# Identity products beside attention's transposes, for the first two units of heads instead of the first five

## The chip, the cores and the metric

The program runs on one core of one Trainium2 chip. The metric is device time in microseconds (us). The core's engines are named as the profile names them: PE (TensorE matmul) with PEld (its weight load), DVE (VectorE), ACT (ScalarE), POOL (GpSimd) and SP (SyncE, which here only issues transfers; its queue is SPq).

## What is computed

Attention with a local or a strided mask, then a two-layer MLP on its output, then a routed mixture of eight experts. Cut to what matters here:

```python
scores = scale * np.matmul(q, k.transpose(0, 1, 3, 2))     # 4 batches, 8 heads, 576 rows, 64 wide
scores = np.where(masks[None], scores, -1e9)               # heads 0-3 local, heads 4-7 strided
attn = np.exp(scores - scores.max(-1, keepdims=True))
attn = attn / (attn.sum(-1, keepdims=True) + 1e-9)
x = np.matmul(attn, v)                                     # to (2304, 512)
h = x @ w_in; x = np.maximum(0.01 * h, h) @ w_out          # w_in 512x2048, w_out 2048x512
out = moe2(x)                                              # 8 experts, capacity 288 tokens each
```

## The kernel before

**Attention.** A unit `u` (0 to 15) is two heads of one batch; `u % 4` below 2 means local heads, else strided ones. Each unit has two groups `g`, and `attention()` walks the 32 pairs (u, g) as a pipeline: at step s it transposes q and k of the next unit (`a_tr`, L122), makes the scores of pair s (`a_qk`, L166, with the mask and minimum on DVE in L157 and the exponential on ACT in L159), normalises them (`a_norm`, the sums on DVE in L178 and L179, the products on POOL in L181), transposes the probabilities of pair s-2 (`a_pt`, L194, for each of the two heads h, copied out of PSUM by ACT in L196) and multiplies those of pair s-3 with V (`a_pv`, L209). q, k and V of later units are loaded through SP's queue (L97, L106 to L110) into buffers that come free when earlier units have been used.

**The identity products.** In `a_pt`, ahead of the transposes of one pair and one head, PE multiplies the identity with itself three times (L192) into `p[:, 3]`, a column block that nothing reads. L193 transposes `n` blocks (3, or 2 for the first strided group) into the blocks below it. Before the change this is done for units 0 to 4. `a_qk` has a like product for units 0 and 1 (L169), which stays. A product of this kind is two instructions in the trace (each fp32 matmul of L192, L122, L166, L194 and L209 runs as two).

**What stands beside it.** From the start, 32 halves of the two MLP weights are loaded by POOL's queue (L306 for `w_in`, L309 for `w_out`, 512 KB each, two buffers) and turned from fp64 into fp32 by ACT (L320) and DVE (L322 to L324): `convert(n)`. When the first eight pairs of attention are written out in the program, the MLP begins: block 0 of tokens, with `g1` (L373 to L375, into the PSUM tile `p1`, one buffer), `g2` (L397 to L399), and `split` (L349 on ACT, L352 on POOL) for the weights' high and low parts; pieces of attention are written between its pieces.

**What sets the order.** Each engine runs its instructions in the order of its own queue. That order isn't the one written: the tile framework's scheduler picks it when the program is built, by its own estimate of durations. So an edit of a few instructions can move their neighbours on every engine.

Of the kernel before, what the change touches and what calls it, by code (L numbers as in the profile page):

```python
# [26 lines left out]
def body(ctx, tc, q, k, v, w_in, w_out, w_gate, w1, w2, out):  # L27
# [109 lines left out]
    def group(u, g):  # L137

        if u % 4 < 2:
            return 96, 128, [(96 * i, 96 * i, ml0 if i == 0 else ml, i) for i in range(3 * g, 3 * g + 3)]  # L140
        w = 18 * RG[2 * g][1]
        return w, w, [(18 * RG[i][0], 32 + 18 * RG[i][0], msf, i) for i in ((0, 1), (2, 3, 4))[g]]
# [41 lines left out]
    def a_pt(u, g, h):  # L184
        nq, nk, tl = group(u, g)
        n = len(tl)
        if h == 0:
            PT[u, g] = at.tile([128, 2, 3, 128], F32, name="pt", tag="pt")
        tag = "p2" if u < 5 and h else "pT"
        p = ps.tile([128, 4, 128], F32, name="pP", tag=tag, bufs=BUFS[tag])  # L190
        for _ in range(3 if u < 5 else 0):
            nc.tensor.matmul(p[:, 3], ident, ident, start=True, stop=True)  # L192
        for i in range(n):  # L193
            nc.tensor.transpose(p[:nk, i, :nq], SC[u, g][0][:nq, h, i, :nk], ident[:nq, :nq])  # L194
        if h or EARLY[0]:
            nc.scalar.activation(PT[u, g][:nk, h, :n, :nq], p[:nk, :n, :nq], AF.Copy)  # L196
        else:
            nc.vector.tensor_copy(PT[u, g][:nk, h, :n, :nq], p[:nk, :n, :nq])
# [40 lines left out]
    def attention():  # L239
# [9 lines left out]
        for s in range(n + 3):  # L249
# [10 lines left out]
            if mid:  # L260
                a_pt(*mid, 0)
                yield
# [12 lines left out]
            if mid:  # L275
                a_pt(*mid, 1)
                yield
# [704 lines left out]
```

## Time and profile before

| | us |
|---|---|
| median of 3 runs | 918.29 (913.65 to 925.14) |
| the profiled execution | 926.83 |
| its span in the trace | 925.1 |
| PE busy in the span | 860.2 (93%) |
| ACT / DVE / POOL busy | 441.9 / 563.3 / 471.5 |

The profiled execution is 8.5 us over the median of the runs, and 1.7 us of it lie around its span. Spans on PE are modelled: an instruction that is shown as 272 ns long is followed by the next of its kind well before those are over, so the cost of a row is better read from one start to the next. [...]

### The profile page before, as it was taken

The page shows a single profiled execution, that of the slowest core. Times are in us where ns is not written, and L with a number is a line of the kernel's source. Part 1 is how long each engine was busy: PE and PEld are TensorE (multiplying, and loading weights), DVE is VectorE, ACT ScalarE, POOL GpSimd, SP SyncE. Part 2 cuts the span into 40 slices and gives each one's busy share as a digit, 9 for nine tenths or more (in the row PEclk, how much of TensorE's full clock was granted, in tenths as well). Part 3 has the DMA queues.
Part 4 walks back from the last instruction along what each step waited for, and adds up shares of the span by engine and source line. Part 5 has one row for each costly group of instructions (what it writes and reads, how often), then busy time and mean ns, then how long its engine had stood idle before and what let it go on. Part 6 is the DMA issues. An engine that isn't in the chain of part 4 may idle for free.

```text
span 925.1 us, 16905 instructions
## 1 busy us (share of the span) xinstructions
PE 860.2 (93%) x6274; PEld 726.1 (78%) x6274; DVE 563.3 (61%) x1543; ACT 441.9 (48%) x1095; POOL 471.5 (51%) x394
## 2 busy tenths in 40 slices
PE   7889998899999999999999999978998989897994
PEld 4777766587887888778898877658998989797994
DVE  6777889856446445554555556566877767675330
ACT  5778667464446445454455423324435434243531
POOL 3645646564555556555655445745446263426621
PEclk9789999999999999999999999987999999798997
DMA  8596554320111100100000002325356362425710
GB/s 183 142 200 157 141 144 124 119 61 5 36 26 53 43 14 2 47 1 1 35 1 1 1 1 80 114 67 177 129 154 185 102 182 95 141 92 154 213 35 26
DMA packets 86450, 80.59 MB, mean 87 GB/s; under 512 B 65376, under 2 KB 65376, under 8 KB 86368
## 3 DMA queue, kind: packets, MB, share of 16 engines
q1 hardware_dynamic: 78688, 53.30, 21.1%
q0 software_dynamic: 7680, 26.22, 9.3%
q8 instruction: 49, 0.80, 0.4%
q14 instruction: 33, 0.27, 0.1%
HBM read 70.06 MB, written 9.44 MB: 86 GB/s over the span
## 4 chain that ended last, share of the span: by engine, by line
PE 64%; DMA 10%; DVE 9%; issue 7%; POOL 4%; ACT 4%; SPq 1%; POOLq 0%; ACTq 0%; DVEq 0%
PE p L373 5%; PE p L397 5%; DMA raw<-in_moe_w_dram 4%; PE p L375 4%; PE p L374 4%; PE p L399 4%; PE p L398 4%; PE g L859 3%; PE g L860 3%; PE g L861 3%; PE p L536 2%; PE q L896 2%; PE p L538 2%; PE pS L166 2%; PE p L537 2%
## 5 line engine op out<-in xcount | busy, mean ns | idle before, releaser
L352 POOL TENSOR_TENSOR lo<-WO,hi 128x512 fp32r<-128x512 f32 x96 | 126.6, 1319 | 95.1 <-ACT hi L349 94.9
L352 POOL TENSOR_TENSOR lo<-WI,hi 128x512 fp32r<-128x512 f32 x96 | 126.9, 1323 | 90.1 <-DVE hi L351 58.3
L801 POOL TENSOR_TENSOR wlo<-raw,whi 128x1024 fp32r<-128x1024 f32 x40 | 95.8, 2410 | 113.9 <-ACT whi L800 113.3
L373 PE MATMUL p<-xh,hi 128*128 128x384 f32 x256 | 98.1, 383 | 5.5 <-DVE g L382 5.5
L349 ACT ACTIVATE hi<-WO 128x512 fp32r<-128x512 f32 x96 | 60.5, 630 | 88.2 <-PE q L898 43.7
L375 PE MATMUL p<-xh,lo 128*128 128x384 f32 x256 | 86.9, 339 | 1.4 <-POOL lo L352 1.4
L800 ACT ACTIVATE whi<-raw 128x1024 fp32r<-128x1024 f32 x64 | 66.1, 1055 | 44.4 <-DMA raw<-in_moe_w_dram 39.2
L374 PE MATMUL p<-xl,hi 128*128 128x384 f32 x256 | 86.6, 338 | 0.6 <-DVE xl L234 0.6
L397 PE MATMUL p<-hi,gh 128*128 128x512 f32 x192 | 82.8, 431 | 0.8 <-ACT gh L383 0.8
L859 PE MATMUL g<-hh,whi 128*128 128x288 f32 x256 | 81.4, 319 | 0.5 <-ACT hh L843 0.5
L860 PE MATMUL g<-hl,whi 128*128 128x288 f32 x256 | 79.0, 309 | 0.1
L861 PE MATMUL g<-hh,wlo 128*128 128x288 f32 x256 | 78.7, 307 | 0.0
L836 PE MATMUL g<-exh,whi 128*128 128x288 f32 x256 | 78.4, 307 | 0.0
L837 PE MATMUL g<-exl,whi 128*128 128x288 f32 x256 | 77.4, 303 | 0.0
L838 PE MATMUL g<-exh,wlo 128*128 128x288 f32 x256 | 77.2, 302 | 0.0
L399 PE MATMUL p<-hi,gl 128*128 128x512 f32 x192 | 75.7, 394 | 1.3 <-DVE gl L384 1.3
L159 ACT ACTIVATE sc<-sc,mx 96x128 f32<-96x128 f32 (+2 forms) x176 | 67.6, 386 | 16.6 <-DVE mx L157 16.6
L398 PE MATMUL p<-lo,gh 128*128 128x512 f32 x192 | 75.2, 392 | 0.0
L373 PEld LDWEIGHTS p<-xh,hi 128*128 128x128 f32 x256 | 48.2, 188 | 16.6 <-DVE g L382 6.8
L181 POOL TENSOR_TENSOR sc<-sc,mx 96x384 f32<-96x384 f32 (+2 forms) x64 | 52.3, 834 | 17.3 <-DVE mx L179 10.2
L381 ACT ACTIVATE g<-p 128x384 f32<-128x384 f32 x64 | 31.1, 486 | 57.0 <-PE p L375 56.7
L351 DVE CAST hi<-WI 128x512 fp32r<-128x512 f32 x59 | 26.8, 454 | 46.1 <-PE p L374 35.9
(203 smaller groups left out, 2257.5 us busy)
## 6 DMA issues: line engine op xcount, KB each, us to landing
raw<-in_moe_w_dram SPq DMA_DIRECT2D x64, 512.0 KB
wraw<-in_moe_w_in_dram POOLq DMA_DIRECT2D x16, 512.0 KB
wraw<-in_moe_w_out_dram POOLq DMA_DIRECT2D x16, 512.0 KB
rawq<-in_q_dram SPq DMA_DIRECT2D x32, 144.0 KB
rawk<-in_k_dram SPq DMA_DIRECT2D x32, 144.0 KB
x2d<-x SPq DMA_DIRECT2D x18, 256.0 KB
vt<-in_v_dram SPq DMA_DIRECT2D x16, 160.0 KB
vt<-in_v_dram SPq DMA_DIRECT2D x48, 27.0 KB
```

The costliest lines, as they stand in the source:

```text
L352: nc.gpsimd.tensor_sub(lo, src, hi.bitcast(F32))
L373: nc.tensor.matmul(p1, wh[:, cs], xh[:, c], start=(c == 0), stop=False)
L374: nc.tensor.matmul(p1, wh[:, cs], xl[:, c], start=False, stop=False)
L375: nc.tensor.matmul(p1, wl[:, cs], xh[:, c], start=False, stop=(c == 3))
L397: nc.tensor.matmul(p2[t], gh[:, s], oh, start=(f == 0), stop=False)
L398: nc.tensor.matmul(p2[t], gh[:, s], ol, start=False, stop=False)
L399: nc.tensor.matmul(p2[t], gl[:, s], oh, start=False, stop=(f == 15))
L801: (nc.vector if n in (1, 5, 7) else nc.gpsimd).tensor_sub(lo, raw, hi.bitcast(F32))
L836: nc.tensor.matmul(p, wh, xh[:, c], start=(c == 0), stop=False)
L859: nc.tensor.matmul(p, wh, hh[:, j], start=(j == 0), stop=False)
L860: nc.tensor.matmul(p, wh, hl[:, j], start=False, stop=False)
L861: nc.tensor.matmul(p, wl, hh[:, j], start=False, stop=(j == 7))
```

## The change

```diff
@@ a_pt(u, g, h)
         tag = "p2" if u < 5 and h else "pT"
         p = ps.tile([128, 4, 128], F32, name="pP", tag=tag, bufs=BUFS[tag])
-        for _ in range(3 if u < 5 else 0):
+        for _ in range(3 if u < 2 else 0):
             nc.tensor.matmul(p[:, 3], ident, ident, start=True, stop=True)
         for i in range(n):
             nc.tensor.transpose(p[:nk, i, :nq], SC[u, g][0][:nq, h, i, :nk], ident[:nq, :nq])
```

For units 2, 3 and 4, two groups and two heads each, three products go: 36 products. The PSUM tile that they wrote keeps its size, its tag and its place. The loads, the transposes and the copies are the same in number.

The order on PE, at the transposes of units 2 and 3 that follow each other some 46 us after the start (L194 with 108 and 126 rows are strided groups; `pT` is a transpose of q or k, `pP` one of probabilities):

```order
-L192 MATMUL pP<-ident 128x128 x3
 L194 MATMUL pP<-ident,sc 108x108 x3
 L122 MATMUL pT<-ident,rawq 128x96 x2
-L192 MATMUL pP<-ident 128x128 x3
 L194 MATMUL pP<-ident,sc 126x126 x2
```

Here two sets of three products are gone and nothing else has moved.

The order on PE a little later, between the product with V of unit 2's second group and that of unit 3's first (`pS` are scores). Before:

```order
L192 MATMUL pP<-ident 128x128
L122 MATMUL pT<-ident,rawq 128x96 x2
L122 MATMUL pT<-ident,rawk 128x96 x2
L166 MATMUL pS_883<-qk 96x128
L166 MATMUL pS_884<-qk 96x128
L166 MATMUL pS_883<-qk 96x128
L166 MATMUL pS_884<-qk 96x128
L192 MATMUL pP<-ident 128x128 x4
L194 MATMUL pP<-ident,sc 108x108 x3
L209 MATMUL pX<-pt,vt 64x126 x4
```

With the change:

```order
L194 MATMUL pP<-ident,sc 128x96 x3
L122 MATMUL pT<-ident,rawq 128x96 x2
L122 MATMUL pT<-ident,rawk 128x96 x2
L166 MATMUL pS_859<-qk 96x128
L194 MATMUL pP<-ident,sc 108x108 x3
L166 MATMUL pS_860<-qk 96x128
L166 MATMUL pS_859<-qk 96x128
L209 MATMUL pX<-pt,vt 64x126 x3
```

Five products are gone from the piece; the transposes of 108 rows have moved ahead of three of the four scores, and those of unit 4's first group and head, which stood below, now stand ahead of the transposes of q and k.

On SP's queue one of two loads of a later unit's q has moved behind the six loads of V that followed it:

```order
-L97 DMA rawq<-in_q_dram 96x6x64 x2
+L97 DMA rawq<-in_q_dram 96x6x64
 L108 DMA vt<-in_v_dram 96x64
```

Behind the first eighty or so microseconds the order of every engine is as it was.

## Rows read from the trace of the kernel before

**Rows 1.** The page's head and the first of its busy times.

```profile
span 925.1 us, 16905 instructions
PE 860.2 (93%) x6274; PEld 726.1 (78%) x6274; DVE 563.3 (61%) x1543; ACT 441.9 (48%) x1095; POOL 471.5 (51%) x394
```

**Rows 2.** Busy time by engine in five stretches, granted clock, DMA share, GB/s.

```profile
core 0: us, PE busy (x) PEld busy (x) DVE busy (x) ACT busy (x) POOL busy (x), PEclk, DMA share, GB/s
40.00:60.00 20.00, 16.81 (x172) 14.20 (x170) 14.10 (x70) 16.31 (x66) 8.40 (x14) 1.00 0.92 208
60.00:74.00 14.00, 13.64 (x101) 10.51 (x101) 10.04 (x39) 10.88 (x40) 6.29 (x9) 0.76 0.66 153
81.00:119.00 38.00, 37.44 (x242) 27.60 (x242) 32.20 (x76) 25.70 (x75) 24.46 (x27) 1.00 0.62 156
126.00:190.00 64.00, 56.28 (x352) 40.76 (x351) 54.98 (x126) 39.30 (x110) 37.31 (x37) 1.00 0.38 111
190.00:560.00 370.00, 368.12 (x2457) 301.59 (x2456) 194.04 (x522) 176.12 (x440) 200.58 (x168) 1.00 0.08 21
```

**Rows 3.** L192 on PE: 40 to 81 us, then the whole span (ns min/median/max).

```profile
L192 PE MATMUL pP<-ident 128*128 128x128 f32 x78 | 13.4, 308 | 0.4 <-ACT qk L133 0.2
...
L192 PE MATMUL pP<-ident x120: 272/275/581, 15.0 to 80.8; 128*128 128x128 f32 x120
```

**Rows 4.** PE in order of time: start, us, instructions [idle before <-releaser].

```profile
46.43 0.94 PE L192 MATMUL pP<-ident 128*128 128x128 f32 x6
...
48.82 0.36 PE L122 MATMUL pT<-ident,rawq 96*128 96x96 f32 x2 [1.17 <-DMA rawq<-in_q_dram]
49.01 0.86 PE L192 MATMUL pP<-ident 128*128 128x128 f32 x6
49.71 0.38 PE L194 MATMUL pP<-ident,sc 126*126 126x126 f32 x2
...
85.62 0.36 PE L122 MATMUL pT<-ident,rawk 96*128 96x96 f32 x2 [0.56 <-DMA rawk<-in_k_dram]
```

**Rows 5.** The chain that ended last, 52 to 86 us: start, us, what.

```profile
52.64 6.52 DMA wraw<-in_moe_w_in_dram
59.18 0.66 ACT cg L320
...
61.40 0.53 PE pP L192 x2
...
63.85 2.00 PE pP L192 x8
...
68.11 0.65 PE pP L192 x2
...
70.44 0.87 PE pP L192 x6
...
73.79 0.76 SPq L106
...
81.39 4.09 DMA rawk<-in_k_dram
```

**Rows 6.** ACT in order of time, 60 to 69 us: instructions that waited.

```profile
60.54 0.40 ACT L159 ACTIVATE sc<-sc,mx 96x128 f32<-96x128 f32 x1 [0.43 <-DVE mx L157]
...
65.07 0.67 ACT L320 ACTIVATE cg<-wraw 128x512 f32<-128x512 f32 x1 [0.51 <-DMA wraw<-in_moe_w_out_dram]
...
66.43 0.44 ACT L196 ACTIVATE pt<-pP 108x324 f32<-108x324 f32 x1 [0.69 <-PE pP L194]
...
67.48 0.44 ACT L233 CAST xh<-pX 128x168 fp32r<-128x168 f32 x1 [0.61 <-PE pX L209]
...
68.58 0.40 ACT L159 ACTIVATE sc<-sc,mx 96x128 f32<-96x128 f32 x1 [0.66 <-DVE mx L157]
```

**Rows 7.** PE in single microseconds: us, busy (x), granted clock, DMA share, GB/s.

```profile
59.00:60.00 1.00, 0.00 (x0) 1.00 0.05 11
61.00:62.00 1.00, 0.85 (x5) 0.86 0.75 111
...
67.00:68.00 1.00, 1.00 (x10) 0.50 0.89 315
68.00:69.00 1.00, 1.00 (x9) 0.72 1.20 250
```

## Prediction

> **What bounds the kernel now.** I began with the page's head: PE is busy for 860.2 of 925.1 us [rows 1], so work taken off PE could be worth its full time, if it is taken where PE is what everything waits for. The next view, busy time by stretch, says where that is. From 190 to 560 us PE is busy for 368.12 of 370 us: nothing there waits for anything but PE. From 81 to 119 us it is much the same, 37.44 of 38. From 126 to 190 us PE stands for 7.7 of 64 us, and DVE is the busier engine in proportion to what it can do, 54.98 of 64 us, so there the conversion of the weights has a say [rows 2]. The change touches none of these stretches. It lies in the 40 us ahead of them, and the question is how much earlier the stretch from 81 us begins.
>
> The group of L192 gives the size: between 40 and 81 us it has 78 instructions. 72 of them go (36 products of two instructions each); the other six belong to unit 1 and stay [rows 3]. In that time there are two parts, which the same two views tell apart. From 40 to 60 us PE is busy for 16.81 of 20 us and ACT for 16.31, and the DMA engines for 0.92 of the time, so PE is not alone in setting the pace. From 60 to 74 us PE is busy for 13.64 of 14 us, ACT for 10.88, and PE's granted clock is 0.76 [rows 2]: there PE is the bound. The chain of waits agrees. At 52.64 us it runs through a transfer of weights of 6.52 us, on which ACT's conversion at 59.18 us stood, then through PE with four pieces of L192, and from 73.79 us through SP's queue and a transfer of k that lands at 85.5 us [rows 5].
>
> **The cost of what goes.** A set of three products, six instructions, starts at 49.01 us, and the next instruction starts at 49.71 us: 0.70 us at the upper clock, 0.117 us for an instruction [rows 4]. Twelve instructions run at the lower clock: their three pieces in the chain are 0.53, 2.00 and 0.65 us, 3.18 together [rows 5]. The other 60 cost 60 x 0.117 = 7.0 us. So 10.2 us of PE's time go. That is 1.1% of 926.83 us, and it is the most that the removal alone could give. What is left of it is worked out by part:
>
> 1. *Before 59 us.* Seven sets (42 instructions, 4.9 us). The first of them stand ahead of a transpose at 48.82 us that had already waited 1.17 us for q [rows 4]; without 0.70 us of products at 46.43 us that wait is 1.87 us, and nothing is earlier. The sets behind it end in front of ACT's conversion at 59.18 us, and that waits for a transfer [rows 5]. The copies that PE's product with V needs stand behind it in ACT's queue. Ends: 0, if that transfer lands when it did; 0.7 us, one set, if its issue, which stands behind other work on POOL and DVE, comes earlier too. I take 0.
> 2. *From 60 to 73 us.* The chain holds four pieces of L192: 0.53 + 2.00 + 0.65 + 0.87 = 4.05 us [rows 5]. All of it would be gained if PE alone set the end. But ACT must do its own work there. Its waits in this part are 0.43 + 0.51 + 0.69 + 0.61 + 0.66 = 2.90 us, of which 0.51 is for a transfer [rows 6]. When the products are gone ACT can close the others, 2.39 us, and then it is what PE waits for. Ends: 0, if DVE and the transfer fill the room; 4.05. I take 2.4, since the four others are for PE or for DVE, which stood on PE's scores.
> 3. *From 73 to 86 us.* Two sets, 1.4 us. Behind 73 us the chain is SP's: ten loads of V at about 0.76 us each, then k, whose transfer takes 4.09 us [rows 5]. PE waited 0.56 us for it at 85.62 [rows 4]. Without the products it waits longer. Ends: 0 and 1.4. I take 0. That the loads begin when PE's product with V of unit 3 is done is why the gain of part 2 survives: SP starts as much earlier.
> 4. *The moved instructions.* The transposes of unit 4 that moved up need POOL's products, which needed ACT's and DVE's work; they are late by some tenths or not at all. One load of q moved behind six of V costs nothing by the time of its use. I take 0, with 0.5 us to either side.
> 5. *Behind 86 us.* From 81 to 119 us PE is full, and DVE has 5.8 us idle [rows 2]. A shift of 2.4 us goes through. From 126 to 190 us DVE has 9 us idle in 64, so I keep all of it, with 0 as the other end.
>
> Sum: 926.83 - 2.4 = 924.4 for the profiled execution; from the median of the runs, 918.29 - 2.4 = **915.9 us**.
>
> **The clock.** At 59 us PE was idle for a whole microsecond; from late in 61 us to the middle of 68 us the granted clock was 0.50 (0.86 in the first of these microseconds, 0.72 in the last: 0.28 + 6 + 0.56 = 6.8 us) [rows 7]. So the products did not keep the clock there: they stand in PE's queue like everything else, wait with it, and at that clock they are themselves the longest thing in it. My sum leaves the lower clock where it was. [...]
>
> **The rivals.**
>
> *A, the forecast:* 1 to 4 us are gained, 914 to 917 us. Half the chance, 0.50.
>
> *B, nothing is gained.* The transfer at 59 us and ACT's queue hold the first part, and in the second the lower clock lasts past 68.6 us, to the end of the stretch. PE's work there without the products is 13.64 - 4.05 = 9.6 us; 6.8 - 3.2 = 3.6 us of that ran at the lower clock already, and the 6.0 others would take 12.0 in the worst case, so 15.6 us against 14. If half of this comes true the gain of part 2 is used up: 918 us. For it speak ACT's 10.88 of 14 us and the conversion's own pace; against it, that PE's queue stays full from 60 us on. 0.22.
>
> *C, slower: the products had held the clock from 40 to 60 us,* where it is 1.00 [rows 2]. PE's work there without them is 16.81 - 4.9 = 11.9 us; at the lower clock all through it is 23.8 us against 20, 3.8 us late, and the second stretch adds 15.6 - 14 = 1.6 by B's sum. That is 5.4 us: 923.7 us. It decides from the point where PE's idle time between 46 and 49 us has brought the clock down and it stays down over 50 us. For it: the gaps grow by as much as the products leave. Against it: in the stretch PE has at least 3 us of slack in front of ACT's wait at 59.18 us, so a short fall is hidden. 0.16. [...]
>
> *D, all of it is gained:* 10.2 us, and 1.8 more (half of 3.6) if the lower clock doesn't come: 918.29 - 12 = 906.3; with 8 us, 910. It needs q, the weights and ACT all to come earlier with PE, against parts 1 and 3. 0.12.
>
> **How the numbers follow.** The likeliest is A with 915.9; I say 916. A, B and most of C lie between 912 and 924. The three runs shown spread over 11.5 us, six times the gain that I forecast, so the range must also hold what differs from run to run: 908.5 to 923.5. That leaves out the lower half of D and the upper end of C, some 2 in 10 together. A alone would be 911 to 921. 2% of the time, about what a measurement of this kernel can tell from no change, is 18.4 us. All of the products are 10.2 us and C is 5.4 us, so no case by itself gets there; 0.03 for faster and 0.02 for slower are for what I don't see.
>
> **What the changed profile would show.** L192 has 48 instructions, the last before 45 us. ACT's conversion still waits for weights near 59 us (part 1), and PE's idle time ahead of it is 3 to 5 us longer. SP's ten loads of V of unit 6, which began shortly before 73.79 us, begin near 71 (part 2), and the wait for k at about 83 us is 1.5 to 2 us long (part 3). From 81 to 119 us all is the same, some 2.4 us earlier. The forecast is wrong if the granted clock falls between 46 and 58 us or stays at 0.50 beyond the loads of V (B, C), or if the weights at 59 us come several us earlier (D).

## The result: 0.7% slower, and the profile after

| | before | with the change |
|---|---|---|
| median of 22 runs, us | 918.33 (913.65 to 928.81) | 926.44 (919.80 to 933.53) |
| ratio, 95% interval | | 1.0072 (1.0045 to 1.0099) |
| the profiled execution, us | 926.83 | 920.40 |

The change makes the kernel slower, in this comparison by 0.0072 x 918.33 = 6.6 us (the medians lie 8.1 us apart). A second comparison on another chip gave 1.0015 (0.9972 to 1.0059), an interval that holds 1, and weighted by their intervals the two give about 1.0056. Runs more than 1.5% above the fastest of their kernel are left out of the ratios and the mean clocks, four of the changed kernel's twelve in the second comparison (its means over all runs stand at 1.0022). The two profiled executions stand the other way round, 926.83 and 920.40 us: single executions spread over 12 us or more, and the profile of before is from the upper end of its runs, the profile of after from the lower end. So the spans of the two traces can't be compared; stretches of them can, and traces of further executions show which of the differences come back.

The page's head and its PE line for the changed kernel, as in [rows 1]; then busy time by engine in the five stretches of [rows 2] (PE, PEld, DVE, ACT, POOL, granted clock, DMA share, GB/s):

```profile
span 918.5 us, 16760 instructions
PE 852.8 (93%) x6202; PEld 718.0 (78%) x6202; DVE 566.0 (62%) x1543; ACT 442.0 (48%) x1095; POOL 471.4 (51%) x394
```

```profile
40.00:60.00 20.00, 14.79 (x146) 11.80 (x144) 14.52 (x69) 16.48 (x66) 9.56 (x15) 0.97 0.87 201
60.00:74.00 14.00, 10.16 (x53) 7.39 (x53) 8.52 (x40) 9.37 (x35) 4.62 (x6) 0.56 0.63 161
81.00:119.00 38.00, 35.39 (x229) 26.87 (x229) 30.50 (x75) 26.91 (x85) 22.12 (x24) 0.99 0.57 139
126.00:190.00 64.00, 54.62 (x330) 39.03 (x331) 55.22 (x123) 39.08 (x113) 33.70 (x36) 0.97 0.48 134
190.00:560.00 370.00, 367.17 (x2437) 301.55 (x2436) 197.30 (x537) 178.62 (x449) 203.34 (x169) 1.00 0.08 21
```

From 190 to 560 us little is new. From 60 to 74 us PE has run 53 matmuls where it had run 101, of which 18 were the products, and the granted clock is 0.56 where it was 0.76. ACT and DVE do less there too, 9.37 and 8.52 us for 10.88 and 10.04. From 81 to 119 us, where nothing was to change, PE is busy for 35.39 us, before for 37.44.

In the trace of before 849 of its 925 whole microseconds read 1.00, 60 read 0.50 and 16 something between; in this one 840 of 918, 63 and 15. 1.00 is the upper clock and 0.50 the lower one of this document. PE of the changed kernel in single microseconds (us, busy, granted clock, DMA share, GB/s), as in [rows 7]:

```profile
60.00:61.00 1.00, 0.00 (x0) 1.00 0.22 48
61.00:62.00 1.00, 0.01 (x1) 0.79 0.03 8
62.00:63.00 1.00, 1.00 (x12) 0.50 0.27 57
...
69.00:70.00 1.00, 1.00 (x7) 0.50 1.15 280
...
80.00:81.00 1.00, 1.00 (x7) 0.50 0.14 32
81.00:82.00 1.00, 0.89 (x11) 0.50 0.17 39
82.00:83.00 1.00, 0.93 (x11) 0.97 0.27 59
```

The clock falls at the same place as before, behind the wait at 59 to 62 us. But it now stays at 0.50 until 82 us: all twenty microseconds from 62 to 82 read 0.50. In the trace of before it was back at 1.00 after 6.8 us. PE in order of time (start, us, instructions, idle before), for the places of [rows 4] and the two products with V of 108 rows that the forecast used as marks:

```profile
50.49 0.36 PE L122 MATMUL pT<-ident,rawq 96*128 96x96 f32 x2 [1.11 <-DMA rawq<-in_q_dram]
...
61.99 1.35 PE L209 MATMUL pX<-pt,vt 108*64 108x108 f32 x12 [3.28 <-ACT pt L196]
...
73.64 0.73 PE L166 MATMUL pS<-qk 64*96 64x128 f32 x2 [1.23 <-DVE mx L157]
...
76.39 1.35 PE L209 MATMUL pX<-pt,vt 108*64 108x108 f32 x12
...
85.08 0.39 PE L397 MATMUL p<-hi,gh 128*128 128x512 f32 x1
...
89.20 0.44 PE L373 MATMUL p<-xh,hi 128*128 128x384 f32 x1 [1.57 <-DVE g L382]
```

The twelve instructions of L209 take 1.35 us in both places; they took 0.78 us before. The waits at 73.64 and 89.20 us, both for DVE, are new. ACT's waits, as in [rows 6]:

```profile
61.01 0.66 ACT L320 ACTIVATE cg<-wraw 128x512 f32<-128x512 f32 x1 [0.64 <-DMA wraw<-in_moe_w_in_dram]
...
63.39 0.52 ACT L233 CAST xh<-pX 128x216 fp32r<-128x216 f32 x1 [0.68 <-PE pX L209]
...
66.82 0.49 ACT L133 ACTIVATE qk<-pT 128x384 f32<-128x384 f32 x1 [0.42 <-PE pT L122]
...
68.20 0.44 ACT L196 ACTIVATE pt<-pP 108x324 f32<-108x324 f32 x1 [0.89 <-PE pP L194]
...
70.74 0.49 ACT L133 ACTIVATE qk<-pT 128x384 f32<-128x384 f32 x1 [1.54 <-PE pT L122]
```

All of these but the first, which is for a transfer, are waits for PE, with the products gone. SP's ten loads of V, which began at 72.91 us before:

```profile
77.81 8.43 SPq L106 DMA_DIRECT2D vt<-in_v_dram  x10
```

### The profile page after: what moved, and what is told of

Its sections match the earlier page's. It is cut to its first block, busy times and chain, and to the rows that moved or that the text cites. A ratio compares the mean times of both kernels' runs of the same rounds, so it can differ in the third digit from the quotient of the medians.

```text
span 918.5 us, 16760 instructions
## 1 busy us (share of the span) xinstructions
PE 852.8 (93%) x6202; PEld 718.0 (78%) x6202; DVE 566.0 (62%) x1543; ACT 442.0 (48%) x1095; POOL 471.4 (51%) x394
## 4 chain that ended last, share of the span: by engine, by line
PE 63%; DVE 11%; DMA 9%; issue 7%; ACT 5%; POOL 4%; SPq 0%; POOLq 0%; ACTq 0%; DVEq 0%
PE p L373 5%; DMA raw<-in_moe_w_dram 4%; PE p L397 4%; PE p L375 4%; PE p L374 4%; PE p L399 4%; PE p L398 4%; PE g L860 3%; PE g L859 3%; PE g L861 3%; PE p L536 2%; PE q L896 2%; PE p L538 2%; DVE cg L323 2%; PE p L537 2%
## 5 line engine op out<-in xcount | busy, mean ns | idle before, releaser
L373 PE MATMUL p<-xh,hi 128*128 128x384 f32 x256 | 98.8, 386 | 8.7 <-DVE g L382 7.6
L375 PE MATMUL p<-xh,lo 128*128 128x384 f32 x256 | 87.6, 342 | 1.6 <-POOL lo L352 1.6
L397 PE MATMUL p<-hi,gh 128*128 128x512 f32 x192 | 82.9, 432 | 0.8 <-ACT gh L383 0.8
L373 PEld LDWEIGHTS p<-xh,hi 128*128 128x128 f32 x256 | 48.9, 191 | 20.9 <-DVE g L382 9.7
```

Source lines behind the costliest of these rows:

```text
L373: nc.tensor.matmul(p1, wh[:, cs], xh[:, c], start=(c == 0), stop=False)
L375: nc.tensor.matmul(p1, wl[:, cs], xh[:, c], start=False, stop=(c == 3))
L397: nc.tensor.matmul(p2[t], gh[:, s], oh, start=(f == 0), stop=False)
```

## Experiments

Two theories were put against each other. **Theory 1, the clock:** in the stretch from 60 to 82 us the products bring TensorE's clock back from 0.50 to 1.00; without them it stays low, and the work on PE takes longer: twice as long at most by an estimate from the two readings, 1.35 us for 0.78 in the twelve instructions of L209. **Theory 2, the order:** the scheduler built another order from the edit, and the moved instructions make PE wait.

One table for all of them. "Mean clock" is the granted clock of the whole program, as a mean over the runs that the ratio counts, and beside it that of the kernel before in the same comparison; a clock lower by 0.010 is some 18 us more at 0.50 (2 x 0.010 x 920), an estimate from the two readings; in the trace of before, with its mean of 0.963, the same sum gives 68 us, and its 60 us at 0.50 and 16 us between come to 68 too. The comparisons were made on several chips, and the mean clock of the kernel before differs between them, so it is the difference in a row that tells. "47 to 60" and "60 to 85" are the granted clocks of these stretches in the kernel's trace, and "last V" is when the last product with V starts in it.

| kernel | of the products of units 2, 3, 4 | order | ratio to before (95%) | mean clock, before's | 47 to 60 | 60 to 85 | last V, us |
|---|---|---|---|---|---|---|---|
| before, two traces | 36 | before | 1 | | 1.00, 1.00 | 0.86, 0.93 | 436.0, 435.7 |
| changed, three traces | none | its own | 1.0072, 1.0015 (above) | 0.9542, 0.9640 (the second) | 1.00, 0.79, 1.00 | 0.59, 0.59, 0.59 | 443.3, 442.4, 443.2 |
| no2 | not unit 2's | own | 1.0014 (0.9978 to 1.0051) | 0.9620, 0.9669 | 0.87 | 0.86 | 439.7 |
| no3 | not unit 3's | own | 1.0068 (1.0029 to 1.0107) | 0.9605, 0.9669 | 0.93 | 0.76 | 443.8 |
| no4 | not unit 4's | own | 0.9986 (0.9947 to 1.0026) | 0.9655, 0.9669 | 1.00 | 1.00 | 436.8 |
| only3 | unit 3's alone | own | 1.0060 (1.0026 to 1.0095) | 0.9521, 0.9640 | 0.84 | 0.59 | 446.9 |
| k1 | 36, one row each | before | 1.0120 (1.0063 to 1.0176) | 0.9514, 0.9669 | 0.73 | 0.50 | 448.7 |
| k1u2 | 36, unit 2's one row | before | 1.0025 (0.9996 to 1.0055) | 0.9625, 0.9659 | 0.74 | 1.00 | 439.3 |
| k1u3 | 36, unit 3's one row | before | 1.0032 (0.9991 to 1.0073) | 0.9584, 0.9640 | 1.00 | 0.59 | 442.1 |
| r128 | 36 in fp32r, short | before | 1.0071 (1.0034 to 1.0109) | 0.9569, 0.9659 | 0.97 | 0.60 | 439.0 |
| r512 | 36 in fp32r, 512 columns | before | 1.0031 (0.9996 to 1.0067) | 0.9605, 0.9659 | 1.00 | 0.93 | 435.4 |
| pv3 | 18, ahead of L209 | own | 1.0102 (1.0067 to 1.0138) | 0.9565, 0.9640 | 0.99 | 0.86 | 441.7 |
| qk5 | none; 10 among the scores | own | 1.0110 (1.0063 to 1.0158) | 0.9545, 0.9685 | 1.00 | 0.58 | 443.3 |
| both5 | 36, and 10 among the scores | own | 1.0003 (0.9962 to 1.0045) | 0.9686, 0.9685 | 1.00 | 1.00 | 438.1 |

### Repeated traces: what comes back (before2, after2, after3)

The kernel before once more, and the changed kernel twice more.

> The kernel before, for a second trace. Theory 1 (the clock): between 45 and 95 us the granted clock is at 0.50 for 3 to 10 us, and the last product with V (L209) starts near 436 us, within 3 us. If instead the lower clock lasts 15 us or more here too, the difference between the first two traces was chance.

> The changed kernel a second time, for a second trace. Theory 1 (the clock): again a stretch of 13 us or more at 0.50 that begins between 52 and 64 us, and a ratio of 1.004 to 1.010. Theory 2 (the order): the same ratio, but the lower clock may be short; the same waits at the moved instructions are seen again (PE for a score at 73.6 us, 1.2 us).

> The changed kernel, for a third trace. Theory 1 (the clock): 15 us or more at 0.50 between 45 and 95 us, and the last product with V near 443 us, within 3 us. Chance: anything from 0 to 20 us.

PE from 60 to 85 us (us, busy, granted clock, DMA share, GB/s), first the two traces of the kernel before, each in its own fence, then the three of the changed kernel:

```profile
60.00:85.00 25.00, 24.06 (x172) 0.86 0.62 151
```

```profile
60.00:85.00 25.00, 22.75 (x172) 0.93 0.59 152
```

```profile
60.00:85.00 25.00, 20.98 (x120) 0.59 0.48 125
```

```profile
60.00:85.00 25.00, 21.46 (x122) 0.59 0.53 137
```

```profile
60.00:85.00 25.00, 21.77 (x123) 0.59 0.52 140
```

It comes back each time. In single microseconds the stretch at 0.50 near 60 us lasts 6.8 and 3.4 us in the traces of before, 20 to 21 us in those of the changed kernel. All the last products with V lie within 1 us for the same kernel, and 7.1 us apart between the two (mean 443.0 and 435.9). That is near the ratio's 6.6 us; of what differs behind that point, where single executions spread, nothing is shown to be the change's. Not all of it agrees: after2's ratio, 1.0015, is below what Theory 1 forecast, and its trace alone of the three has two more stretches at 0.50, 42 to 49 and 56 to 59 us:

```profile
47.00:60.00 13.00, 11.12 (x91) 0.79 0.93 202
```

The second trace of before supplies the marks once more (start, us, PE):

```profile
61.03 0.78 PE L209 MATMUL pX<-pt,vt 108*64 108x108 f32 x12 [1.56 <-ACT pt L196]
...
71.58 0.78 PE L209 MATMUL pX<-pt,vt 108*64 108x108 f32 x12
...
79.05 0.40 PE L397 MATMUL p<-hi,gh 128*128 128x512 f32 x1
```

### One unit's products out (no2, no3, no4, only3)

```diff
-        for _ in range(3 if u < 5 else 0):
+        for _ in range(3 if u < 5 and u != 2 else 0):     # no2; 3 and 4 alike
+        for _ in range(3 if u < 2 or u == 3 else 0):      # only3
```

> Only unit 2's twelve products go; those of units 3 and 4 stay. Theory 1 (the clock: the products of units 3 and 4, which stand in the stretch that begins at the lower clock near 61 us, brought the clock back after 7 us; without them it stays at 0.50 to 82 us): unit 2's products stood before 59 us, at 1.00, so the clock comes back near 69 us as before, and the time is that of the kernel before, ratio 0.998 to 1.002. Theory 2 (the order: the scheduler's moved instructions make PE wait): the order built for this kernel is nearer to that of the changed kernel than to that of before, so the ratio is 1.004 to 1.010.

> Only unit 3's twelve products go. Theory 1 (the clock): the products that stood near 61 to 66 us are gone, those of unit 4 behind them stay, so the lower clock lasts some us longer than 7, and the ratio is 1.002 to 1.006. Theory 2 (the order): the order built for this kernel differs from both others by much; no clear forecast, with the clock as before.

> Only unit 4's twelve products go. Theory 1 (the clock): three of the four sets of products from 64 to 81 us are gone, so the lower clock lasts longer than 7 us, and the ratio is 1.002 to 1.007. Theory 2 (the order): the order built for this kernel is near to that of before, so the ratio is 0.998 to 1.002 and the clock is back near 69 us.

> Of units 2 to 4 only unit 3 keeps its products; 24 of the 36 go. Theory 1 in the form that unit 3's products are the ones that count: ratio 0.996 to 1.002. Theory 1 in the form that it is their number in the stretch from 46 to 80 us that counts: half of the loss or more, 1.003 to 1.007. Theory 2 (the order): its order stands some fifty rows from either kernel's; no forecast.

Unit 2's and unit 4's products can each go at no measurable cost; unit 3's can't, 1.0068. But unit 3's alone don't do it either: only3 is at 1.0060 with the clock at 0.59 from 60 to 85 us. So the first reading of no3, that one unit's products are the ones that count, failed with only3. How many of them must stand where isn't shown. no2's ratio fits Theory 1, and it speaks against Theory 2: its order on PE and DVE is nearer to the changed kernel's than to before's. no4 is a miss of Theory 1, which had forecast a longer fall and 1.002 to 1.007; Theory 2 had its ratio right. The fall that unit 4's products would have had to end didn't come: its trace has 1.00 from 42 to 86 us, and the two products with V of 108 rows are 8.6 us apart (62.18 and 70.77 us), where the traces of before have 11.9 and 10.6. Each of these kernels has an order of its own, though, so they can't separate the two theories.

### The same order, less work in the products (k1, k1u2, k1u3)

```diff
-            nc.tensor.matmul(p[:, 3], ident, ident, start=True, stop=True)
+            nc.tensor.matmul(p[:, 3], ident[:128 if u < 2 else 1], ident[:128 if u < 2 else 1], ...)   # k1
+            # k1u2, k1u3: one row for u == 2 (u == 3) alone
```

> The products of units 2 to 4 stay, in number and in the order of every engine as in the kernel before, but each multiplies one row instead of 128 (the identity's first row with itself), so that only one of the array's 128 rows has work while as many columns pass. Theory 1 (the clock) in the form that the work in the array holds the clock: the lower clock lasts to 80 us or longer, and with the products' own time still spent the ratio is 1.006 to 1.014. Theory 1 in the form that it is enough that PE has something to run: as before, 0.998 to 1.002. Theory 2 (the order): as before, 0.998 to 1.002.

> All products stay, in the order of the kernel before on every engine; only unit 3's twelve use one row of the array instead of 128. Theory 1 (the clock, and what unit 3's products do in it, since taking them out alone cost 0.7% and taking unit 2's or unit 4's out alone cost nothing): ratio 1.003 to 1.010, lower clock for 13 us or more from about 55 us. Theory 2 (taking unit 3's out cost 0.7% because the order built without them was another one): ratio 0.998 to 1.002.

> The order of the kernel before; only unit 2's twelve products use one row of the array instead of 128, as unit 3's did in an earlier run. Theory 1 (the clock, decided by what stands behind 59 us): mean granted clock within 0.004 of the kernel before, ratio 0.998 to 1.003. If it is the number of full products anywhere from 41 to 81 us that counts: as unit 3's, clock 0.006 lower, ratio 1.002 to 1.006.

Every engine has the order of the kernel before. L192 in the whole trace of k1 (ns min/median/max of both forms together, first and last start):

```profile
L192 PE MATMUL pP<-ident x120: 270/372/582, 15.1 to 92.9; 1*128 1x128 f32 x72, 128*128 128x128 f32 x48
```

and PE (us, busy, granted clock, DMA share, GB/s) in some stretches of k1, and in the fence behind it from 60 to 85 us in k1u3:

```profile
47.00:60.00 13.00, 13.00 (x90) 0.73 0.68 169
52.00:53.00 1.00, 1.00 (x9) 0.97 1.25 262
53.00:54.00 1.00, 1.00 (x4) 0.50 0.83 278
60.00:85.00 25.00, 25.00 (x135) 0.50 0.43 115
87.00:88.00 1.00, 1.00 (x9) 0.96 0.24 54
```

```profile
60.00:85.00 25.00, 24.33 (x141) 0.59 0.45 112
```

Two sets of six instructions in k1u3, of 128 rows and of one, and what follows them, at the upper clock:

```profile
49.91 0.86 PE L192 MATMUL pP<-ident 128*128 128x128 f32 x6
50.61 0.38 PE L194 MATMUL pP<-ident,sc 126*126 126x126 f32 x2
...
57.55 0.93 PE L192 MATMUL pP<-ident 1*128 1x128 f32 x6
58.41 0.49 PE L194 MATMUL pP<-ident,sc 108*108 108x108 f32 x3
```

From the start of a set to what follows it takes 0.86 us with one row and 0.70 us with 128 (0.67 and 0.77 in other places): at most 2.3 us over k1's twelve sets, of the 11 us that it loses. Nothing has moved, and PE is busy for all of the time from 47 to 85 us; yet the clock, back at 1.00 since 46 us, falls at 53 us and is 0.50 until 87. So k1 shows two things: without full products the clock comes back late, here after 34 us, and it fell without a wait, where the kernel before, with a wait of 1.17 us at 48.82 us [rows 4], stayed at 1.00. k1 is 1.2% slower, more than the changed kernel, as was forecast of a kernel that has the lower clock and still spends the products' time. With unit 3's products alone at one row the trace has 20 us at 0.50 and the last product with V 6.2 us late; its ratio, 1.0032, has an interval that still holds 1. For unit 2's the clock from 60 to 85 us is 1.00, but 7 us at 0.50 stand ahead of it, from 51 to 58 us; the last product with V is 3.4 us late, and the ratio's interval just holds 1. Its ratio lies in both forecasts of k1u2, so it doesn't choose between them. Theory 2 forecast no loss for k1 and k1u3: k1's interval excludes that, k1u3's doesn't.

### The same order, with half of the products' instructions (r128, r512)

```diff
-            nc.tensor.matmul(p[:, 3], ident, ident, start=True, stop=True)
+            nc.tensor.matmul(p[:, 3], *[ident if u < 2 else idr] * 2, ...)            # r128; idr: the identity in fp32r
+            # r512, for u >= 2: p as 512 columns <- idr, idr four times side by side
```

What was open by now was how much of the loss is the order's: every kernel that had lost products had also been ordered anew.

> The order of the kernel before on every engine (one copy of the identity into fp32r is added at the start). The 36 products of units 2 to 4 run in fp32r, 128 columns in one instruction instead of two, so most of their time on PE goes (about 7 of 10 us, by the step of 0.175 us that the 384-column fp32r products of L373 to L375 show) and nothing has moved. Theory 1 (the clock): the lower clock from about 60 us lasts 13 us or more, the mean granted clock falls to 0.954 to 0.960, the last product with V starts 3 us or more behind 436, ratio 1.002 to 1.009. Theory 2 (the order makes the loss, PE's time is a gain): mean clock as before, ratio 0.994 to 0.999.

> As r128 in order and in fp32r, but each of the 36 products passes 512 columns (the identity four times), 0.2 us or so each, near to what two fp32 instructions took. Theory 1 (the clock): PE has as much to run as before, the mean granted clock is that of the kernel before within 0.003, ratio 0.996 to 1.003. If fp32's two passes are what counts: as r128.

L192 of units 2 to 4 and, in the fence behind it, PE from 60 to 85 us, in r128:

```profile
L192 PE MATMUL pP<-idr x36: 220/306/474, 41.5 to 83.2; 128*128 128x128 f32 x36
```

```profile
60.00:85.00 25.00, 24.52 (x145) 0.60 0.51 137
```

36 instructions instead of 72 (half of the products' time, not the 7 of 10 us that were expected, since one takes 0.12 us, 0.37 us for three from 56.56 to 56.93 us, where one of fp32 takes 0.117 us [rows 4]), one copy of the identity more on DVE, and nothing moved: the clock is 0.60, the mean clock of the runs 0.9569 against 0.9659, and the ratio 1.0071. By its runs that is as large a loss as the changed kernel's, with the order of the kernel before. So less work in the products is enough to lose the clock and the time; another order isn't needed for it. Its trace has less of the loss by 440 us, though: the last product with V is 3.1 us late, where the changed kernel's are 7.1 us late. r512 gave the work back: its trace is that of the kernel before (0.93, last product with V at 435.4), but over its runs the mean clock is 0.9605, between r128 and before and below what was forecast, and 1.0031 isn't told apart from 1. It doesn't decide whether one such instruction makes up for two of fp32.

### Products in other places (pv3, qk5, both5)

```diff
-        p = ps.tile([128, 3 * 126], F32, name="pX", tag=tag, bufs=BUFS[tag])   # pv3: in a_pv, ahead of L209
+        p = ps.tile([128, 512], F32, name="pX", tag=tag, bufs=BUFS[tag])
+        for _ in range(3 if 2 <= u < 5 else 0):
+            nc.tensor.matmul(p[:, 384:], ident, ident, start=True, stop=True)
-            if u < 2 and i:                                                    # qk5, both5: in a_qk
+            if u < 5 and i:
```

pv3 and qk5 have `range(3 if u < 2 else 0)` in a_pt, both5 has the line of before.

> The products of units 2 to 4 stand ahead of the products with V, not of the transposes: three for each pair, 18 in place of 36, into a column block of the product's own tile that nothing reads. They run while PE waits for the copies of the probabilities. Theory 1 (the clock): activity in those waits holds the clock or brings it back, so the ratio is 0.992 to 1.002, below the changed kernel's in any case. Theory 2 (the order): no forecast of its own; as the changed kernel, 1.004 to 1.010, if what counts is what was moved.

> The changed kernel, with the products that stand among the scores (L169, two for each pair, until now for units 0 and 1) for units 0 to 4: twelve products instead of the 36, in another place. Theory 1 (the clock, any array work in the stretch counts): the mean granted clock of the runs comes up from 0.954 to 0.957 or more, and the ratio to the kernel before is 0.998 to 1.005, below the changed kernel's. Theory 2 (the order or the place alone): as the changed kernel or worse, 1.004 to 1.010, with any clock.

> The kernel before with the products among the scores for units 0 to 4 too: twelve more products than before. Theory 1 (the clock): the mean granted clock of the runs is at or above that of the kernel before on the same chip, by 0.000 to 0.006; the products cost about 3 us of PE and give back as much, ratio 0.995 to 1.003. If PE's time were what counts, not its clock: 1.002 to 1.005 with the same clock.

Neither place serves. (The products among the scores of units 2 to 4 are ten, not the twelve of the expectations: a strided first group has two blocks and so one product.) qk5 has the clock of the changed kernel from 60 to 85 us and is at 1.0110, so Theory 1 in the form that any work on PE serves is a miss. pv3 is a miss that the clock doesn't explain: 0.86 from 60 to 85 us and 0.9565 in the mean, above the changed kernel's 0.9542, but a time that is worse, 1.0102. Its order is far from both others, so Theory 2 may hold for it; that stays open. both5, ten more products than before, has the clock of the kernel before and its time within 0.5%. Of all kernels run, none is faster than the kernel before beyond its interval.

## Why the prediction was wrong

The forecast was 915.9 us, between 908.5 and 923.5; the median is 926.44.

**The step that failed is the clock's.** The prediction said that "the products did not keep the clock there", since they stood in the stretch at 0.50 and were the longest things in it, and so the "sum leaves the lower clock where it was". The trace had been read for what makes the clock fall, the wait at 59 us. It hadn't been asked what brings the clock back. The products that ran at the lower clock, the costliest pieces of the chain, 3.18 us for twelve [rows 5], belong to what ended it: with one row in place of 128 in the same instructions, in the same order, it lasts 34 us (k1; with unit 3's alone 20 us, k1u3). So the same rows that were counted as a gain of 3.18 us were the price of getting 1.00 back 14 to 17 us sooner. Nor is the wait all that makes the clock fall: k1's fell at 53 us, and PE hadn't waited.

Point by point, with three traces of the changed kernel against two of before:

1. *Before 59 us: nothing gained.* Right. The weights that ACT's conversion waits for came no earlier (61.01 us, before 59.18). The first product with V of 108 rows starts at 61.99, 61.58 and 61.28 us, before at 60.16 and 61.03. PE's wait ahead of it grew from 1.30 and 1.56 us to 3.28, 1.95 and 3.98: what the products left was idle, as forecast, though by less than the 3 to 5 us that it named.
2. *From 60 to 73 us: 2.4 us gained.* Wrong in sign. From that product with V to the next one of 108 rows it took 11.9 and 10.6 us, and takes 14.4, 13.8 and 13.8. ACT didn't close its waits; it got new ones for PE, 0.42 to 1.54 us each. The 2.4 us of waits weren't gained; the part became 1.9 to 3.8 us longer, at the lower clock.
3. *From 73 to 86 us: nothing, since SP's loads hold the end.* The sign of the shift was wrong here too: the loads began at 77.81 us, not near 71, and the forecast wait for k near 83 us isn't there, because PE came late. From the second product with V to the first of L397 it takes 8.7, 9.3 and 9.2 us, before 7.5 in both traces, the clock being at 0.50 until 82 to 84 us.
4. *The moved instructions: nothing.* This isn't borne out. In all three traces of the changed kernel PE has two waits for DVE that it has in neither trace of before: 1.23 us for a score's tile (at 73.64 us in the first trace), and 1.44 to 1.57 us ahead of L373 (at 89.20 us). k1, k1u3 and r128, which have the order of before and are late too, have neither. r128 loses as much by its runs without a moved instruction, but by 440 us its trace has lost 3.1 us of the changed kernel's 7.1. So the clock is a cause, and how much of the loss is the order's stays open.
5. *Behind 86 us a shift goes through.* Right, to the wrong side: first L397 4.8 to 6.0 us late, last product with V 6.4 to 7.6.

Two sums of it were off, and neither moves the forecast: the runs' spread of 11.5 us is 4.8 times 2.4, not six times, and the lower half of D and the upper half of C are 1.4 in 10 by their chances, not 2.

**The rivals.** C had the right mechanism, products that hold the clock (with one row in them 0.50 from 60 to 85 us, k1, with 128 rows 0.86 and 0.93), but mostly at another place. It put the fall from 40 to 60 us, where the changed kernel's clock is low in one of three traces (0.79 from 47 to 60 us, 1.00 in the others); k1 and k1u2, in the order of before, fall there too (0.73 and 0.74). That its price, 5.4 us, is near the measured one is luck, as 3.8 us of it are for that stretch. B had the right place, a lower clock that lasts beyond 68.6 us, but let it end with the stretch at 74 us and set it off against a gain that didn't come. Together they had 0.38, and should have been one rival with the larger chance. Each was held down with an argument that doesn't bear: C with the slack in front of 59 us, which is on the wrong side of the fall; B with "PE's queue stays full from 60 us on", while k1 shows a PE that is busy for 25 of 25 us at 0.50. Both counted work at 0.50 at twice its time, an estimate from the two readings; the twelve instructions of L209 took 1.7 times theirs (1.35 us for 0.78).

**Idle time and the clock.** Near 60 us the five traces agree: 1.3 to 4.0 us of idle PE and then 0.50, while no4, where PE waited 0.88 us there, has no fall. Elsewhere idle time alone doesn't settle it: after3 waited 2.10 us at 49.70 us and stayed at 1.00 until 62, and k1 fell at 53 us without a wait. What ran at 0.50 for 20 us in the changed kernel are transposes, scores, products with V and a few of the MLP's products (L373 to L375); no run shows what any one of these does to the clock.

## What to carry to other kernels

Here work on TensorE that nobody reads was not only a cost: without it the kernel was slower by a ratio of 1.0072. Before such work is taken out, find the stretches where the clock is low, and ask of each what makes it fall and what brings it back; here what brought it back were the very instructions that looked longest there, 3.18 us for twelve [rows 5]. And when an edit also lets a scheduler order anew, keep the order fixed in an experiment, by an instruction of the same kind that does less work, before the order is blamed or cleared.

## What the runs showed of the hardware

- From 60 to 85 us PE was busy by the profile for 25 of 25 us and at 0.50 all the time (k1); with the same instructions in the same order, but 128 rows in the products, it was back at 1.00 after 3.4 and 6.8 us (the two traces of before). The clock of k1 also fell, at 53 us, while PE was busy for 13 of 13 us.
- A set of three identity products of one row took 0.86 us to the start of what follows, a set of 128 rows 0.67 to 0.77 us (k1u3, at 1.00): fewer rows didn't make it shorter.
- Three fp32r products of 128 columns, three instructions, took 0.37 us to the start of what follows (56.56 to 56.93 us in r128, at 1.00), three fp32 ones, six instructions, 0.70 us [rows 4].
- The mean granted clock of the program, set against that of the kernel before in the same comparison, told slower kernels from others better than one profile did. It is lower by 0.0064 to 0.0155 in the six kernels of the experiments whose ratio is above 1 by its interval, by 0.0056 at most in the others; only the changed kernel's second comparison, 0.0098 and 1.0015, stands apart. The changed kernel's first trace had the shorter span, by 6.6 us.
